# Asking for four experts' weights at other places of one DMA queue

## The chip, the cores and the metric

The kernel runs on one core of one Trainium2 chip. The metric is device time in microseconds (us) for one execution; lower is better. Engines are named as in the profile: PE (TensorE matmuls), PEld (TensorE weight loads), DVE (VectorE), ACT (ScalarE), POOL (GpSimd) and SP (SyncE, which here does little but ask for DMAs). SPq and POOLq are the DMA-asking parts of SP and POOL.

## The reference, cut to what matters

```python
# 1. global filter: x is (8, 2496, 256)
X = np.fft.rfft(x, axis=1)
y = np.fft.irfft(X * (filt_r + 1j * filt_i)[None], n=2496, axis=1)
# 2. mixture of experts over all 19968 rows of y; 8 experts, capacity 80
logits = y @ w_gate
expert_idx = np.argmax(logits, axis=1)
gate_w = softmax(logits)[arange(N), expert_idx]
for e in range(8):
    tok = rows with expert_idx == e, the 80 with the largest gate_w
    h = np.maximum(y[tok] @ w1[e], 0.0)            # w1[e]: 256 x 1024
    out[tok] = gate_w[tok, None] * (h @ w2[e])     # w2[e]: 1024 x 256
```

All other rows of the output are zero. One expert's two weight matrices are 2 x 1024 KB in float32.

## The kernel before, in words

The Fourier transform is done by matmuls in two stages. For each of the 8 batches b the filtered spectrum is written to DRAM (`yf[b]`) and the gate's logits are computed from it. Only some rows of the inverse transform are ever needed, at most 80 for each expert, so the kernel first finds the kept rows (on DVE) and then inverts just those.

That is done in seven **inverse rounds**, the list `ROUNDS`, 0 to 6. A round makes 128 rows of `y`. Its left operand is a tile `wt`: rows of a table of cosines, fetched from DRAM by four indirect DMAs on POOL's queue (`gather_rows`, tile `gt`, L852) and transposed on DVE (`turn_rows`, L863). Its right operand is a **page**, the spectrum of one batch, read back from `yf` by `load_page` (four DMAs, L837). Round r below 4 uses page r. Rounds 4 to 6 are cut into four groups of 32 rows: round 4 uses pages 4 and 5, round 5 pages 5 and 6, round 6 page 6 and the last batch's spectrum, which never left the core. `fill(n)` writes n of a round's 20 steps to PE (L875): one matmul of 128 columns a step in rounds 0 to 3, four of 32 columns from round 4 on. When a round's last step is done, `fill` copies the result on ACT to a tile `yr` (L881; round 5 goes to the tile `z`) and asks on SP's queue for its store to `y_sel` in DRAM (L882). `yr` has a single buffer, so the next round's copy waits for the store before it.

The eight experts come last. The rows of each are gathered from `y_sel` (L1155 for the first two, L1182 for the others, on POOL's queue), turned on PE, and run through `layer1` (L1215, `ph`) and `layer2` (L1235, `po`), then turned back (L1251), scaled by the gate on ACT (L1260) and scattered to the output (L1171).

`load_weights(e)` asks on SP's queue for expert e's weights with two DMAs, w1 (L1064) and w2 (L1066), below w0, w1, ... for expert 0, 1, ... as a whole. The five tiles that hold them are mostly the places of pages: w0 has a place of its own, w1 takes page 3's place, w2 page 4's, w3 page 5's, w4 page 6's; a request for one waits until the last round that reads the page is done. w5, w6 and w7 are asked for after layer 2 of experts 0, 1 and 2.

The order of the program text sets the order on every engine and queue (`tc.manual_schedule()`). SP takes its requests strictly one after the other: while one waits, all behind it wait.

## Time and profile before

| | us |
|---|---|
| median of 3 runs | 378.23 |
| lowest and highest run | 378.18, 383.19 |
| profiled execution, its own time | 379.92 |
| span of its trace | 378.1 |
| PE busy in the span | 351.0 (93%) |

The profiled execution took 1.69 us longer than the median, and 1.8 us of it lie outside the span. Times of day below ("at 288 us") count from the span's start. The inverse rounds fill some 235 to 318 us, the experts 318 to 370 us.

### The profile page before, as it was taken

Reading aid. Unit: us, or ns where it says so; the run is one execution under the profiler, and the core shown is the slowest. Engines: PE = TensorE matmul, PEld = TensorE weight load, DVE = VectorE, ACT = ScalarE, POOL = GpSimd, SP = SyncE. Lnnn points to the kernel's source line nnn. Section 1 sums busy time; section 2 is a strip of 40 time slices with the busy share of each in tenths; the row PEclk is TensorE's granted clock in tenths of the full one; section 3 lists DMA queues with packets and bytes.
Section 4 is the critical chain, followed back from the end, with each engine's and each line's share of the span. In section 5 each row is a group of like instructions: output and inputs, shape, how many; then the busy total and the mean of one; then the engine's idle time right before and its main releaser. Section 6 shows DMA issues by size and latency. Waiting matters only on the chain. (4 is left out here: it accounts for less than half of the span.)

```text
span 378.1 us, 9670 instructions
## 1 busy us (share of the span) xinstructions
PE 351.0 (93%) x3941; PEld 311.2 (82%) x3941; DVE 240.1 (63%) x494; ACT 132.8 (35%) x275; POOL 181.3 (48%) x250
## 2 busy tenths in 40 slices
PE   8888999999999999999999998998897989897990
PEld 4788989989989899899899897697784756786880
DVE  6049666757868858879989889769959540111110
ACT  1545545454545454454444465140100000010110
POOL 8337555544655536636457858850085102223120
PEclk9999999999999999999999999999999999999997
DMA  7998699979988999989989999799999773999310
GB/s 220 287 324 275 190 341 291 341 253 316 344 257 291 332 317 309 372 235 285 353 286 279 395 298 341 261 404 392 413 398 408 272 248 70 346 366 368 106 33 12
DMA packets 41099, 109.92 MB, mean 291 GB/s; under 512 B 4202, under 2 KB 14312, under 8 KB 39176
## 3 DMA queue, kind: packets, MB, share of 16 engines
q1 hardware_dynamic: 36534, 95.94, 74.7%
q0 software_dynamic: 4240, 13.15, 9.6%
q8 instruction: 33, 0.54, 0.6%
q10 hardware_dynamic: 274, 0.14, 0.2%
q14 instruction: 18, 0.15, 0.1%
HBM read 70.42 MB, written 40.37 MB: 293 GB/s over the span
## 5 line engine op out<-in xcount | busy, mean ns | idle before, releaser
L359 POOL TENSOR_TENSOR yt<-p 128x256 f32<-128x256 f32 x156 | 113.3, 748 | 89.7 <-DVE p L351 86.4
L351 DVE TENSOR_TENSOR p<-pb,ft 128x1024 f32<-128x1024 f32 x80 | 96.9, 1214 | 39.2 <-issue 17.9
L316 PE MATMUL pa<-wf_t,x 117*128 117x120 f32 x704 | 90.5, 275 | 2.5 <-DMA x<-in_x_dram 2.5
L316 PEld LDWEIGHTS pa<-wf_t,x 117*128 117x128 f32 x704 | 84.6, 192 | 3.7 <-issue 1.9
L341 PE MATMUL pb<-d_t,t 128*128 128x128 f32 x640 | 84.7, 275 | 1.7 <-ACT t L334 1.7
L341 PEld LDWEIGHTS pb<-d_t,t 128*128 128x128 f32 x640 | 77.7, 192 | 2.2 <-ACT t L334 2.2
L321 ACT COPY tt<-pa 128x480 f32<-128x480 f32 x96 | 47.8, 515 | 78.2 <-PE pa L316 76.0
L875 PE MATMUL pr<-page,wt 128*32 128x256 f32 (+1 forms) x520 | 63.9, 380 | 2.1 <-issue 2.1
L875 PEld LDWEIGHTS pr<-page,wt 128*32 128x32 f32 (+1 forms) x520 | 46.1, 134 | 15.7 <-issue 3.8
L334 ACT COPY t<-pt 128x512 f32<-128x512 f32 x80 | 47.2, 589 | 15.6 <-PE pt L330 13.8
L330 PE MATMUL pt<-ident,tt 128*128 128x128 f32 x320 | 48.6, 274 | 0.4 <-ACT tt L321 0.4
L372 DVE STREAM_TRANSPOSE u<-yt 128x512 f32<-128x512 f32 x70 | 48.9, 699 | 0.0
L852 POOL DMA_INDIRECT gt<-rows_tbl,idxr x28 | 29.4, 1052 | 33.7 <-DVE idxr L694 19.0
L330 PEld LDWEIGHTS pt<-ident,tt 128*128 128x128 f32 x320 | 37.2, 142 | 1.9 <-issue 1.2
L863 DVE STREAM_TRANSPOSE wt<-gt 128x640 f32<-128x640 f32 x28 | 22.4, 827 | 8.2 <-DMA gt<-rows_tbl,idxr 8.1
L1215 PE MATMUL ph_True<-xs_True,w 128*64 128x80 f32 x512 | 20.7, 234 | 1.5 <-issue 1.5
L395 PE MATMUL pz<-yt,wg 128*32 128x512 f32 (+1 forms) x256 | 21.7, 436 | 0.4 <-POOL yt L359 0.4
L1171 POOL DMA_INDIRECT out_dram<-ys_True,idxs x7 | 6.5, 933 | 31.7 <-ACT ys_True L1260 31.7
L1235 PE MATMUL po_True<-hT_True,w 128*64 128x80 f32 x448 | 18.3, 235 | 3.5 <-issue 3.5
L1215 PEld LDWEIGHTS ph_True<-xs_True,w 128*64 128x64 f32 x512 | 19.2, 137 | 2.4 <-issue 2.3
L881 ACT COPY yr<-pr 128x256 f32<-128x256 f32 x6 | 2.3, 379 | 53.6 <-DMA y_sel<-yr 38.4
L1235 PEld LDWEIGHTS po_True<-hT_True,w 128*64 128x64 f32 x448 | 16.6, 137 | 4.7 <-issue 4.2
(226 smaller groups left out, 287.6 us busy)
## 6 DMA issues: line engine op xcount, KB each, us to landing
out_dram<-zero_t SPq DMA_DIRECT2D x32, 624.0 KB
yf<-u SPq DMA_DIRECT2D x56, 320.0 KB
w<-in_moe_w_dram SPq DMA_DIRECT2D x16, 1024.0 KB
page<-yf SPq DMA_DIRECT2D x24, 640.0 KB
x<-in_x_dram SPq DMA_DIRECT2D x16, 936.0 KB
x<-in_x_dram SPq DMA_DIRECT2D x7, 702.0 KB
page<-yf POOLq DMA_DIRECT2D x4, 640.0 KB
fst<-in_filt_r_dram SPq DMA_DIRECT2D x10, 128.0 KB
```

Of the source, the lines that this page charges most:

```text
L316: nc.tensor.matmul(out=ps[:, j, :], rhs=wf_t, start=True, stop=True, lhsT=xt[3 * b + ch][:, j0 + j - JC * ch, 128 * cb:128 * cb + 128])
L321: nc.scalar.copy(out=tt[h][:, :, H3 * j0:H3 * j0 + hn * jn].rearrange("p s (j h) -> p s j h", h=hn), in_=v)
L330: nc.tensor.transpose(ps[:, i, :], tt[h][:, 2 * s:2 * s + 2, :].rearrange("p r n -> p (r n)"), ident[:])
L334: nc.scalar.copy(out=t2[k][:], in_=ps[:])
L341: nc.tensor.matmul(out=ps[:, :, i, :], lhsT=t[:, i, :], rhs=d_t[:, SG * g + i, :], start=True, stop=True)
L351: nc.vector.tensor_tensor(out=p[:], in1=f.unsqueeze(2).to_broadcast(shape), op=AL.mult, in0=ps[:].rearrange("p r s q -> p r (s q)").unsque ...
L359: eng.tensor_tensor(out=y[:, :, 2 * r:2 * r + 2, :], in0=a, in1=b, op=op)
L372: nc.vector.transpose(uu[h][:, :, SG * g:SG * g + SG, :].rearrange("p a s w -> p s a w"), spectrum(h)[:, SG * g:SG * g + SG])
L852: nc.gpsimd.indirect_dma_start(out=gts[b, g][:].rearrange("p s q -> p (s q)"), out_offset=None, in_=quarters, in_offset=bass.IndirectOffse ...
L875: nc.tensor.matmul(st["po"][c:c + w, :], lhsT=wts[r][:, s, c:c + w], rhs=yt_t[:, :, s] if b == B - 1 else columns(pages[b], s), start=(s = ...
L1215: nc.tensor.matmul(ph[c:c + 64, i, 0:cap], lhsT=w1[:, k, f:f + 64], rhs=xs[:, k, :], start=(k == 0), stop=(k == NDB - 1))
L1235: nc.tensor.matmul(po[c:c + 64, d, 0:cap], lhsT=w2[:, fc, 128 * d + c:128 * d + c + 64], rhs=hT[:, fc, :], start=(fc == 0), stop=(fc == NF ...
```

## The change

Three calls of `load_weights` move in the program text; nothing is added or taken away. The request for w0 moves from in front of round 0 to behind round 3, w1's from behind page 5 to behind round 4, and w3's from behind round 6 to behind the store of round 5. w2 and w4 keep their place.

```diff
         load_page(3, last)
-        load_weights(0)
         for g in range(3):
...
         fill(13)
         load_page(5, pg_p)
-        load_weights(1)
         turn_last(7)
...
         fill(20)
+        load_weights(0)
         turn_all(4)
...
         fill(20)
+        load_weights(1)
         load_weights(2)
...
         fill(10)
+        load_weights(3)
         turn_all(6)
...
         fill(20)
-        for e in (3, 4):
-            load_weights(e)
+        load_weights(4)
```

SP's queue, the only engine whose order changes, from the request for page 3 to the request for w2, before. The rows of L1064 and L1066 are w0, w1 and w2 in turn, those of L882 the stores of rounds 0 to 4, the two L837 rows after the first are pages 4 and 5:

```order
L837 DMA page_2954<-yf_148 128x1280 x4
L1064 DMA w_2959<-in_moe_w_dram 128x2x1024
L1066 DMA w_2959<-in_moe_w_dram 128x8x256
L882 DMA y_sel<-yr_3103 128x256
L837 DMA page_3106<-yf_149 128x1280 x4
L882 DMA y_sel<-yr_3228 128x256
L837 DMA page_3231<-yf_150 128x1280 x4
L1064 DMA w_3236<-in_moe_w_dram 128x2x1024
L1066 DMA w_3236<-in_moe_w_dram 128x8x256
L882 DMA y_sel<-yr_3404 128x256
L882 DMA y_sel<-yr_3458 128x256
L882 DMA y_sel<-yr_3588 128x256
```

The same stretch after:

```order
L837 DMA page_2954<-yf_148 128x1280 x4
L882 DMA y_sel<-yr_3100 128x256
L837 DMA page_3103<-yf_149 128x1280 x4
L882 DMA y_sel<-yr_3225 128x256
L837 DMA page_3228<-yf_150 128x1280 x4
L882 DMA y_sel<-yr_3398 128x256
L882 DMA y_sel<-yr_3452 128x256
L1064 DMA w_3455<-in_moe_w_dram 128x2x1024
L1066 DMA w_3455<-in_moe_w_dram 128x8x256
L882 DMA y_sel<-yr_3585 128x256
L1064 DMA w_3588<-in_moe_w_dram 128x2x1024
L1066 DMA w_3588<-in_moe_w_dram 128x8x256
```

Pages 4 and 5 and the stores of rounds 0 to 3 now stand ahead of all weights; w0 stands between the stores of rounds 3 and 4, w1 behind that of round 4, and w2 right behind w1.

The end of the same queue before, from w2 on; `z` is the store of round 5, the `yr` behind it that of round 6, and `bad` is a flag that every engine reads for the branch at the end:

```order
L1064 DMA w_3591<-in_moe_w_dram 128x2x1024
L1066 DMA w_3591<-in_moe_w_dram 128x8x256
L1377 TENSOR_LOAD bad
L1377 ISA x2
L882 DMA y_sel<-z 128x256
L882 DMA y_sel<-yr_3844 128x256
L1064 DMA w_3847<-in_moe_w_dram 128x2x1024
L1066 DMA w_3847<-in_moe_w_dram 128x8x256
L1064 DMA w_3850<-in_moe_w_dram 128x2x1024
L1066 DMA w_3850<-in_moe_w_dram 128x8x256
```

And after:

```order
L1064 DMA w_3591<-in_moe_w_dram 128x2x1024
L1066 DMA w_3591<-in_moe_w_dram 128x8x256
L882 DMA y_sel<-z 128x256
L1064 DMA w_3748<-in_moe_w_dram 128x2x1024
L1066 DMA w_3748<-in_moe_w_dram 128x8x256
L1377 TENSOR_LOAD bad
L1377 ISA x2
L882 DMA y_sel<-yr_3847 128x256
L1064 DMA w_3850<-in_moe_w_dram 128x2x1024
L1066 DMA w_3850<-in_moe_w_dram 128x8x256
```

w3 now stands between the stores of rounds 5 and 6, and the read of the flag comes behind it.

## Rows read from the trace of the kernel before

**Rows 1.** The page: busy time of PE and of its weight loads, share of the span and instructions; then tenths in 40 slices of 9.45 us (PEclk is the granted TensorE clock, DMA the share of the DMA engines); then the queue that brings instructions: packets, MB, share.

```profile
PE 351.0 (93%) x3941; PEld 311.2 (82%) x3941; DVE 240.1 (63%) x494; ACT 132.8 (35%) x275; POOL 181.3 (48%) x250
...
PEclk9999999999999999999999999999999999999997
DMA  7998699979988999989989999799999773999310
...
q8 instruction: 33, 0.54, 0.6%
```

**Rows 2.** Busy time by stretch, 239 to 370 us: stretch, its length, then busy us and instructions of PE, PEld, DVE, ACT and POOL, granted clock, DMA share, GB/s.

```profile
248.00:260.00 12.00, 10.74 (x66) 9.47 (x66) 9.75 (x28) 5.35 (x11) 3.50 (x4) 1.00 1.02 401
260.00:268.00 8.00, 7.98 (x47) 6.94 (x46) 7.23 (x38) 0.00 (x0) 0.00 (x0) 1.00 1.05 392
...
286.00:292.00 6.00, 3.87 (x62) 1.95 (x54) 5.36 (x17) 0.00 (x0) 3.63 (x4) 1.00 1.03 406
...
303.00:306.00 3.00, 1.94 (x25) 1.28 (x29) 1.73 (x6) 0.37 (x1) 0.00 (x0) 1.00 0.30 92
306.00:312.00 6.00, 6.00 (x119) 3.63 (x112) 2.83 (x6) 0.37 (x1) 0.00 (x0) 1.00 0.98 344
312.00:318.00 6.00, 6.00 (x116) 3.49 (x106) 0.00 (x0) 0.00 (x0) 1.91 (x2) 1.00 0.16 46
...
321.00:327.00 6.00, 4.68 (x114) 4.13 (x110) 0.49 (x1) 0.87 (x2) 2.83 (x3) 1.00 0.99 340
327.00:331.00 4.00, 4.00 (x111) 3.82 (x108) 1.14 (x3) 0.00 (x0) 0.00 (x0) 1.00 1.03 341
331.00:352.00 21.00, 17.93 (x437) 16.70 (x433) 3.55 (x10) 3.19 (x8) 5.75 (x6) 1.00 1.06 364
```

**Rows 3.** SP's queue in order of time: start, us (how long the request was held), what; the rows of L1064 and L1066 are w0, w1, w2, then w5.

```profile
244.13 0.40 SPq L1064 DMA_DIRECT2D w<-in_moe_w_dram  x1
...
254.40 7.04 SPq L882 DMA_DIRECT2D y_sel<-yr  x1
261.55 1.93 SPq L837 DMA_DIRECT2D page<-yf  x4
...
285.73 0.38 SPq L1064 DMA_DIRECT2D w<-in_moe_w_dram  x1
...
304.74 0.39 SPq L1064 DMA_DIRECT2D w<-in_moe_w_dram  x1
...
330.07 0.37 SPq L1064 DMA_DIRECT2D w<-in_moe_w_dram  x1
```

**Rows 4.** ACT's copies of rounds 1 and 3: start, us, what, and in brackets the idle time before it and what ended it.

```profile
268.36 0.37 ACT L881 COPY yr<-pr 128x256 f32<-128x256 f32 x1 [12.31 <-DMA y_sel<-yr]
...
301.68 0.37 ACT L881 COPY yr<-pr 128x256 f32<-128x256 f32 x1 [24.17 <-DMA y_sel<-yr]
```

**Rows 5.** PE in round 4, order of time, the last two of its three waits there: start, us, what, number of matmuls, and the idle time before with what ended it ("issue" where the profile shows nothing).

```profile
290.12 0.42 PE L875 MATMUL pr<-page,wt 128*32 128x256 f32 x2 [0.83 <-issue]
291.56 6.24 PE L875 MATMUL pr<-page,wt 128*32 128x256 f32 x107 [1.03 <-issue]
```

**Rows 6.** PE from the first turn of an expert's rows to layer 1 of experts 0 and 1, the same columns; the last and longest of the four waits there.

```profile
318.04 0.45 PE L1193 MATMUL px_True<-ident,xg_first 80*128 80x80 f32 x2
...
320.38 2.57 PE L1215 MATMUL ph_True<-xs_True,w 128*64 128x80 f32 x66
...
325.35 1.96 PE L1215 MATMUL ph_True<-xs_True,w 128*64 128x80 f32 x50 [0.43 <-issue]
```

**Rows 7.** PE in experts 1 to 4, the same columns: the five rows with a wait.

```profile
335.09 0.64 PE L1235 MATMUL po_True<-hT_True,w 128*64 128x80 f32 x13 [0.42 <-issue]
...
336.10 2.30 PE L1215 MATMUL ph_True<-xs_True,w 128*64 128x80 f32 x59 [0.17 <-issue]
...
341.70 0.78 PE L1235 MATMUL po_True<-hT_True,w 128*64 128x80 f32 x17 [1.02 <-issue]
...
348.32 0.98 PE L1235 MATMUL po_True<-hT_True,w 128*64 128x80 f32 x22 [1.47 <-issue]
...
354.06 1.19 PE L1235 MATMUL po_True<-hT_True,w 128*64 128x80 f32 x28 [0.59 <-issue]
```

**Rows 8.** Busy time by stretch, from the end of one wait of rows 7 to the end of the next; columns as in rows 2.

```profile
335.09:341.70 6.61, 5.43 (x127) 4.98 (x127) 1.08 (x3) 0.91 (x2) 2.13 (x3) 1.00 1.06 368
341.70:348.32 6.62, 5.15 (x127) 4.87 (x127) 1.08 (x3) 0.91 (x2) 2.07 (x3) 1.00 1.05 360
348.32:354.06 5.74, 5.14 (x127) 4.86 (x127) 1.08 (x3) 0.91 (x2) 1.08 (x2) 1.00 0.73 253
```

**Rows 9.** DMA queues in the stretches 339.0 to 339.5, 345.5 to 346.0 and 351.5 to 352.0, in this order: the row of the queue that brings instructions (packets, MB, share).

```profile
q8 instruction: 1, 0.02, 14.5%
...
q8 instruction: 1, 0.02, 15.5%
...
q8 instruction: 1, 0.02, 13.1%
```

**Rows 10.** POOL's queue, order of time: the first of three gathers for round 6 that follow each other during round 4, the gather for expert 0, and the first of three for experts 2 to 4.

```profile
286.95 1.00 POOL L852 DMA_INDIRECT gt<-rows_tbl,idxr  x1 [0.30 <-DVE hit L725]
...
314.92 0.96 POOL L1155 DMA_INDIRECT xg_first<-y_sel,idxg  x1 [17.46 <-DMA y_sel<-z]
...
321.15 0.94 POOL L1182 DMA_INDIRECT xg_True<-y_sel,idxg  x1 [4.01 <-PE px_True L1195]
```

## The prediction, made before the changed kernel was run

> **What bounds the kernel now.** I read the page first: PE is busy 93% of the span at a granted clock that is full almost everywhere [rows 1], and the DMA engines run at 0.7 to 0.9 or more in nearly every slice. So I looked for the places where PE, the busy engine, waits, and for what. The table by stretch [rows 2] is the second view. From 248 to 268 us the DMA engines are full (1.02 and 1.05) and PE still runs: 10.74 of 12.00 us, then 7.98 of 8.00. The stretches that stand out are 286 to 292 (PE 3.87 of 6.00), 321 to 327 (4.68 of 6.00) and 331 to 352 (17.93 of 21.00), with a full DMA in all three. In the order of time [rows 5, 6, 7] none of the waits there is for data: each reads "issue", nothing that the profile can name.
>
> The waits of 331 to 352 have a pattern. From the wait that ends at 335.09 to that at 341.70, from there to 348.32 and on to 354.06, PE runs 127 matmuls and as many weight loads each time [rows 7, 8]. One packet of the instruction queue lies in each of these stretches, two to three us before PE goes on [rows 9]. The page has 33 such packets with 0.54 MB, 16 KB each, for 3941 matmuls and as many weight loads [rows 1], 239 of these instructions to a packet, which agrees with 127 matmuls and their loads. I take it that PE stands still because its next block of instructions comes late when the weights fill the DMA engines. From 312 to 318, with the DMA at 0.16, PE does not wait; but from 306 to 312, in rounds 5 and 6 with the DMA at 0.98 from w2, it does not wait either (6.00 of 6.00) [rows 2]. The reason that I see is pace: there 119 matmuls take 6 us, one block lasts over 6 us; in the experts a block lasts some 5 us (5.15 busy of 6.62) [rows 8].
>
> The waits of rows 5 and 6 look different: a few matmuls, a pause, a few more. Both lie in a full DMA just after POOL has begun to ask for three gathers in a row (286.95 and 321.15) [rows 10]. I have no cause for them.
>
> **The change part by part.** All 2 x 1024 KB of each expert are still moved. At the 364 GB/s of 331 to 352 [rows 2] that is 5.8 us of full DMA for each.
>
> *w0 leaves the stretch before 268.* It is asked for at 244.13, and the store of round 0 behind it is held 7.04 us, so that page 4 is asked for at 261.55 only [rows 3]. Without it page 4 goes out up to 7 us sooner, page 5 some 3 us, since round 1's copy on ACT (268.36) had waited for that store [rows 4]. PE gets nothing: it hardly waited from 260 to 268 (7.98 of 8.00) [rows 2]. Term: 0. DVE waits less for gathers in rounds 4 and 5, which is worth nothing while PE is behind it.
>
> *w0 takes w1's place.* Round 3 ends at 285.7, when w1 was asked for [rows 3]; now w0 goes out there, about 1 us later, behind a store. The stream of pages and gathers in front of it is shorter by one expert's 5.8 us. The first use of w0 is at 320.38 [rows 6], over 30 us later. The pauses of round 4 cost 6.00 - 3.87 = 2.13 us of idle PE [rows 2, 5]; the same three gathers and again a new stream of weights meet there, so I leave them as they are: 0, with bounds of 2.13 gained and, from the other such place, 6.00 - 4.68 = 1.32 lost [rows 2, 6].
>
> The Trainium skill ("DMA: Bandwidth & Descriptors", Rules for kernel authors) speaks against this part: it says to ask for a DMA early, compute, and wait for it late. By that rule the later request costs whatever of the transfer is then seen; the trace leaves it over 30 us of cover, so the sum would be the same 0.
>
> *w1 joins w2 behind round 4.* Both go out at about 298.5 instead of 285.73 and 304.74 [rows 3]. They make 11.6 us of full DMA, to some 310, where the share was down to 0.30 from 303 to 306 [rows 2]. PE is in rounds 5 and 6 then. The nearest row is 306 to 312: same rounds, full DMA, no wait. Term: 0; bound above: three blocks of instructions pass from 299 to 320, each late by up to the 1.02 of rows 7, so 3.1 us lost.
>
> *w3 goes out behind round 5*, at about 310.5, into the stretch 312 to 318 whose share was 0.16. Behind it on SP wait the flag's read and round 6's store, which is ready only when the first turn has begun (318.04) [rows 6], after w3's 5.8 us. Round 5's store now queues behind w1 and w2 instead of w2; both orders are through by 310 to 312, so the first gather (314.92) [rows 10] is no later, and its rows are first used at 318.04 [rows 6]. Term: 0.
>
> *What is left for the experts.* In the kernel before, w3 and w4 start together at 319 to 321 and run without a break into w5, w6 and w7 until 352. Now w4 alone runs, 321 to 327. From 327 to w5's data, a little after its request at 330 [rows 3], the DMA rests, where the share was 1.03 [rows 2]. A block of instructions that PE asks for there comes in time: the waits that end at 335.09 and 336.10 go, 0.42 + 0.17 = 0.59 us. From then on w5, w6 and w7 follow each other as before, one each 6.6 us with 5.8 us of stream [rows 8]: the waits of 1.02 and 1.47 stay. The stream ends earlier, since w5 no longer queues behind w3 and w4, by two to three us; then the last wait, 0.59, goes too. The pauses of rows 6 fall in 321 to 325, when one weight stream and three gathers run in both orders: they stay, bound 1.32 gained.
>
> Sum: 0.59 + 0.59 = 1.2 us gained. Against the profiled execution's own 379.92 that gives 378.7; taken from the median, 378.23 - 1.2 = **377.0 us**.
>
> **The rivals.**
>
> *Nothing moves: 378.2 us.* The waits are not from the DMA's load, or they only change places. For it: PE never waits for a byte of weights or pages in these stretches, and the amount of DMA stays the same. Against it: the four waits of rows 7 sit in the full stretch, and none in 312 to 318. The Trainium skill ("Runtime: NRT & Kernel Launch", Instruction fetch mechanics) says that engines take their instructions in 16 KiB blocks, the next while one runs, and that crossing a block is mostly hidden. The block's size agrees with the page's 0.54 MB in 33 packets; that it is hidden does not agree with the 1.02 and 1.47 us of rows 7.
>
> *The pauses go too: 374.7 us.* If the pauses in round 4 and in layer 1 need a queue as deep as before (pages, w0's backlog and w1; w3 with w4 behind it), they shrink: up to 2.13 + 1.32 = 3.45 us more than my sum, 373.6 us at best; two thirds of it gives 374.7. For it: w0's 5.8 us are gone from the backlog at 288. Against it: the share of the DMA, not the depth, is what the rows show, and it stays full.
>
> *Slower: 380.7 us.* Rounds 5 and 6 lose what the experts lost. From 298 to 318 the DMA is now full for 17 of 20 us. The block of instructions must come within the 6 to 7 us in which PE uses one up; in the experts it took about 5 + 1.47 us at the worst [rows 7, 8]. If w1 and w2 together, asked for without a pause, make it 8 us, each of three blocks is late by 1 to 1.5 us: 3 to 4 us lost, less the 1.2 gained, 380.0 to 381.1. It decides at a delay of some 6.5 us, and the trace has that value on the edge. For it: that edge. Against it: the quiet of 306 to 312 with w2 alone.
>
> **How the numbers follow.** Forecast (375.5 to 378.0): 0.45. Nothing moves (378.0 to 378.6): 0.18. Pauses go (372.5 to 375.5): 0.17. Slower (378.6 to 382): 0.20. The range leaves out the lower third of the third case and a little under half of the last, with some allowance for several effects at once: 373.4 to 380.6. A change of 2% is 7.6 us, and about what a measurement here tells from no change. All the idle PE of rows 5 to 7 together is 2.13 + 1.32 + 3.67 = 7.1 us, less than that, so faster by over 2% needs more than everything: 0.03. Slower by over 2% needs a stage to wait for its weights, which have tens of us of cover: 0.03. Within 2%: 0.94.
>
> **What would show it.** In the changed profile: page 4 asked for at about 255 and round 3's copy at about 286 instead of 301.68; DMA share near 1 from 298 to 310, high from 312 to 318, and low from 327 to 331; in PE's order of time no "issue" wait near 335 and a smaller one near 354, still two of 1 us or more between; pauses in round 4 and in layer 1 as before. I am wrong if PE shows "issue" waits between 299 and 318 (the slower rival), if the pauses of round 4 vanish (the faster one), or if layer 1 of an expert waits for its weights, which no part of the sum has.

## The result, and the profile after

The changed kernel is **slower: 1.0063 times the time before, interval 1.0042 to 1.0084**; medians 382.19 us and 379.55 us, 20 runs each. The kernel before took 379.55 in these runs and not the 378.23 from which the prediction started; on that base the ratio gives 380.6 us. The forecast was 377.0, a gain of 1.2 us, so the sign is wrong. The change moves three requests, w0, w1 and w3, not the four of the title. Runs over 1.5% longer than the fastest of the same kernel are left out of the ratios. The profiled execution took 382.2 us, its span is 380.4.

The two traces of the prediction's places, and one more execution of each kernel (its times in the last column), cut at the starts of matmuls:

| stretch | before | after | difference | second pair |
|---|---|---|---|---|
| start of the span to round 0 | 235.56 | 234.82 | -0.74 | +0.93 |
| round 0 to the last matmul of round 6 | 82.17 | 80.56 | -1.61 | -0.87 |
| from there to the first turn of an expert's rows | 0.31 | 4.63 | **+4.32** | **+4.17** |
| first turn to layer 2 of expert 0 | 9.09 | 9.62 | +0.53 | +0.57 |
| layer 2 of expert 0 to the last matmul group | 38.54 | 36.66 | -1.88 | -1.42 |
| last matmul group to the end | 12.46 | 14.12 | **+1.66** | **+1.32** |
| span | 378.1 | 380.4 | +2.3 | +4.7 |

The first row is the same work in both kernels and shows how much two executions differ. Of the two gains, that of the experts was foreseen and that of the rounds put at 0; the two losses are where nothing was looked for.

Of the page, the rows of [rows 1]: PE is as busy as before, and the granted clock has a dip in the two slices of 314 to 333 us.

```profile
PE 352.1 (93%) x3941; PEld 311.6 (82%) x3941; DVE 241.6 (64%) x494; ACT 133.1 (35%) x275; POOL 180.5 (47%) x250
...
PEclk9999999999999999999999999999999998799997
```

Busy time by stretch after, columns as in [rows 2]:

```profile
286.00:292.00 6.00, 6.00 (x116) 3.61 (x112) 4.28 (x14) 0.00 (x0) 2.53 (x3) 1.00 1.02 403
292.00:298.00 6.00, 4.62 (x74) 2.41 (x70) 4.15 (x16) 0.37 (x1) 0.99 (x1) 1.00 1.04 380
...
306.00:312.00 6.00, 6.00 (x120) 3.60 (x112) 0.49 (x2) 0.37 (x1) 0.00 (x0) 1.00 1.02 363
312.00:316.00 4.00, 3.76 (x72) 1.99 (x64) 0.00 (x0) 0.10 (x1) 0.97 (x1) 1.00 0.99 353
316.00:320.00 4.00, 0.00 (x0) 0.02 (x1) 0.00 (x0) 0.27 (x1) 0.95 (x1) 1.00 0.78 216
320.00:323.00 3.00, 2.99 (x16) 3.00 (x16) 0.33 (x1) 0.00 (x0) 1.69 (x2) 0.57 1.03 390
323.00:327.00 4.00, 4.00 (x58) 3.85 (x59) 0.33 (x1) 0.44 (x1) 1.15 (x2) 0.50 0.70 213
327.00:331.00 4.00, 4.00 (x110) 3.91 (x107) 0.98 (x2) 0.44 (x1) 0.00 (x0) 0.97 0.00 0
```

The quiet stretch of the kernel before, 312 to 318 at a share of 0.16 [rows 2], is gone: 0.99. Then PE does nothing for four microseconds, and the seven after them run at a granted clock of 0.57 and 0.50, the lower of its two levels (1.2 GHz). The rest comes at 327 to 331 instead, where the share is 0.00.

What PE waits for there, in its order of time (columns as in [rows 5]); the first row is round 4, the next two round 5, the fourth the first turn, the last two experts 2 and 3:

```profile
285.76 7.09 PE L875 MATMUL pr<-page,wt 128*32 128x256 f32 x128
...
294.49 0.62 PE L875 MATMUL pr<-page,wt 128*32 128x256 f32 x2 [0.37 <-DVE wt L863]
296.13 4.50 PE L875 MATMUL pr<-page,wt 128*32 128x256 f32 x74 [1.02 <-DVE wt L863]
...
320.01 0.42 PE L1193 MATMUL px_True<-ident,xg_first 80*128 80x80 f32 x2 [4.25 <-DMA xg_first<-y_sel,idxg]
...
323.24 6.56 PE L1215 MATMUL ph_True<-xs_True,w 128*64 128x80 f32 x128
...
342.60 0.78 PE L1235 MATMUL po_True<-hT_True,w 128*64 128x80 f32 x17 [0.58 <-issue]
...
349.49 0.98 PE L1235 MATMUL po_True<-hT_True,w 128*64 128x80 f32 x22 [1.74 <-issue]
```

4.25 us before the first turn, for the gather of the first experts' rows. How the gather came late is in two queues. SP's queue after (as [rows 3]; page 4, w0, then the store of round 5 and the first half of w3 behind it):

```profile
253.12 1.80 SPq L837 DMA_DIRECT2D page<-yf  x4
...
285.05 0.40 SPq L1064 DMA_DIRECT2D w<-in_moe_w_dram  x1
...
307.62 0.34 SPq L882 DMA_DIRECT2D y_sel<-z  x1
308.05 0.39 SPq L1064 DMA_DIRECT2D w<-in_moe_w_dram  x1
```

and POOL's two gathers for experts 0 and 1 after (as [rows 10]):

```profile
314.96 0.97 POOL L1156 DMA_INDIRECT xg_first<-y_sel,idxg  x1 [17.62 <-DMA y_sel<-z]
316.23 0.95 POOL L1156 DMA_INDIRECT xg_first<-y_sel,idxg  x1 [0.30 <-issue]
```

The same three requests before, from SP's and from POOL's queue:

```profile
309.96 0.34 SPq L882 DMA_DIRECT2D y_sel<-z  x1
```

```profile
316.19 0.95 POOL L1155 DMA_INDIRECT xg_first<-y_sel,idxg  x1 [0.30 <-issue]
```

Round 5's result is stored 2.34 us earlier than before (307.62 for 309.96), yet the first gather, which waits for the store, goes out at 314.96 as it did at 314.92: the store takes 7.34 us to the gather instead of 4.96. The landings in the trace say why these two times agree: in both kernels the store stands behind w2 and lands 0.34 to 0.36 us after w2's second half (before 313.70 and 314.06, after 313.76 and 314.10). w1, in front of w2, had landed at 307.63.

From the second gather's request to the first turn it is 3.78 us instead of 1.85, and PE, 2.35 us ahead by then, has run out of work. The 1.85 is only a bound, since PE was busy until then. The packets of POOL's queue show the gathers themselves, 48 packets for each, from the first one's request to 317.30, before and then after:

```profile
q0 software_dynamic: 48, 0.07, 11.5%
```

```profile
q0 software_dynamic: 32, 0.05, 7.8%
```

Before, the first gather is complete by 317.27, 2.35 us after its request and some 0.8 us before PE needs it; after, its last part lands at 319.88, 4.92 us after its request, beside w3.

The second loss is in the last scatters, each of which waits for the one before it to land. After, POOL's last three scatters, and ACT's results for the last two of them:

```profile
363.22 0.91 POOL L1171 DMA_INDIRECT out_dram<-ys_True,idxs  x1 [3.01 <-ACT ys_True L1260]
367.27 0.91 POOL L1171 DMA_INDIRECT out_dram<-ys_True,idxs  x1 [3.14 <-DVE hT_True L1221]
372.26 0.91 POOL L1171 DMA_INDIRECT out_dram<-z,idxs  x1 [4.08 <-POOLq L1383]
```

```profile
365.19 0.47 ACT L1260 ACTIVATE ys_True<-pb_True,gate 80x256 f32<-80x256 f32 x1
370.01 0.47 ACT L1260 ACTIVATE z<-po_True,gate 80x256 f32<-80x256 f32 x1 [4.35 <-PE po_True L1244]
```

and POOL's three before:

```profile
362.60 0.91 POOL L1171 DMA_INDIRECT out_dram<-ys_True,idxs  x1 [3.08 <-ACT ys_True L1260]
365.68 0.91 POOL L1171 DMA_INDIRECT out_dram<-ys_True,idxs  x1 [2.17 <-ACT ys_True L1260]
370.13 0.91 POOL L1171 DMA_INDIRECT out_dram<-z,idxs  x1 [3.54 <-ACTq L1383]
```

The requests stand 4.05 and 4.99 us apart instead of 3.08 and 4.45, and the last one goes out 1.78 us after its rows are ready (370.48). No weights move in that stretch.

### The profile page after: what moved, and what is told of

Its sections match the earlier page's. It is cut to its first block, busy times and chain, and to the rows that moved or that the text cites. A ratio compares the mean times of both kernels' runs of the same rounds, so it can differ in the third digit from the quotient of the medians.

```text
span 380.4 us, 9670 instructions
## 1 busy us (share of the span) xinstructions
PE 352.1 (93%) x3941; PEld 311.6 (82%) x3941; DVE 241.6 (64%) x494; ACT 133.1 (35%) x275; POOL 180.5 (47%) x250
## 5 line engine op out<-in xcount | busy, mean ns | idle before, releaser
L875 PEld LDWEIGHTS pr<-page,wt 128*32 128x32 f32 (+1 forms) x520 | 44.5, 134 | 16.5 <-DVE wt L863 2.3
L395 PE MATMUL pz<-yt,wg 128*32 128x128 f32 (+1 forms) x256 | 21.6, 436 | 0.4 <-POOL yt L359 0.4
L1215 PEld LDWEIGHTS ph_True<-xs_True,w 128*64 128x64 f32 x512 | 20.4, 148 | 0.3 <-issue 0.2
L395 PEld LDWEIGHTS pz<-yt,wg 128*32 128x32 f32 x256 | 8.7, 109 | 12.3 <-issue 7.0
```

The lines of the kernel that those rows point to most:

```text
L395: nc.tensor.matmul(out=ps[32 * j:32 * j + 32].rearrange("p (s w) -> p s w", s=pn), lhsT=wg[:, cb, :], rhs=yt_t[:, (2 * b + cb) % 2, 5 * j ...
L875: nc.tensor.matmul(st["po"][c:c + w, :], lhsT=wts[r][:, s, c:c + w], rhs=yt_t[:, :, s] if b == B - 1 else columns(pages[b], s), start=(s = ...
L1215: nc.tensor.matmul(ph[c:c + 64, i, 0:cap], lhsT=w1[:, k, f:f + 64], rhs=xs[:, k, :], start=(k == 0), stop=(k == NDB - 1))
```

## The experiments

**The theory** after the result: w3 took the quiet of 312 to 318 from the chain store of round 5, gather, first turn. **Rivals:** the store queues behind the weights on SP and would be quick on another queue; w2, not w3, is what delays it; w0 or w1 at their new places cost the time; the drop of the clock, not the wait, is the price. All times of the table are from the profiled execution, the ratios from the runs (of e13 and e14 there is one each). "Store" is from the request of round 5's store to the first gather, "gather" from the second gather's request to the first turn (where "turn" is 0.31 or 0.35, PE was busy until then, and the gather may have landed earlier), "turn" from the last matmul of round 6 to the first turn, "end" from the last matmul group to the end of the span.

| kernel | ratio to before | store | gather | turn | end |
|---|---|---|---|---|---|
| before | 1 | 4.96 | 1.85 | 0.31 | 12.46 |
| after | 1.0063 [1.0042, 1.0084] | 7.34 | 3.78 | 4.63 | 14.12 |
| e1_z_act | 1.0069 [1.0036, 1.0102] | 6.87 | 4.85 | 5.23 | 14.13 |
| e2_w2_late | 1.0091 [1.0060, 1.0122] | 2.64 | 5.91 | 2.06 | 13.41 |
| e3_busy | 1.0033 [1.0003, 1.0063] | 8.49 | 4.14 | 6.14 | 13.73 |
| e4_w3_back | 1.0039 [1.0011, 1.0067] | 6.66 | 1.36 | 1.53 | 13.77 |
| e5_only_w0 | 1.0215 [1.0181, 1.0249] | 6.75 | 1.35 | 1.60 | 13.89 |
| e6_only_w1 | 1.0016 [0.9987, 1.0046] | 5.31 | 1.49 | 0.31 | 12.58 |
| e7_only_w3 | 1.0060 [1.0028, 1.0093] | 4.99 | 4.93 | 3.12 | 12.58 |
| e8_quiet | 1.0038 [1.0008, 1.0068] | 2.60 | 4.31 | 0.31 | 14.06 |
| e9_pool6 | 1.0081 [1.0050, 1.0111] | 7.22 | 3.80 | 4.53 | 12.46 |
| e10_act6 | 1.0037 [1.0003, 1.0071] | 7.78 | 3.80 | 5.10 | 12.59 |
| e11_dve6 | 1.0033 [1.0001, 1.0065] | 6.90 | 3.83 | 4.24 | 12.60 |
| e12_pe20 | 1.0120 [1.0074, 1.0166] | 6.23 | 5.06 | 4.80 | 12.60 |
| e13_after | (383.97 us) | 6.42 | 4.56 | 4.48 | 13.78 |
| e14_before | (379.26 us) | 4.87 | 2.08 | 0.31 | 12.46 |
| e15_w3_back_dve6 | 1.0021 [1.0001, 1.0042] | 5.46 | 1.38 | 0.35 | 12.46 |

### Which part of the change it is

**w3 alone** (the kernel before, with w3 behind round 5):

```diff
+        load_weights(3)
         turn_all(6)
...
-        for e in (3, 4):
-            load_weights(e)
+        load_weights(4)
```

> The kernel before with w3's request alone moved, to behind the store of round 5. Rounds 3 and 4 are untouched, so round 6 ends near 318 as before. Theory C: w3 now runs from about 311 to 318 beside the gather of the first experts, whose rows come 2 to 3 us later than in the kernel before; PE waits 2 to 4 us before the first turn and may fall to the lower clock: 1 to 4 us more than the kernel before. If only the depth of the queue in front of round 5's store counts (w1 and w2), nothing is lost here, and the wait near 335 goes: 0.5 to 1.5 us less than the kernel before.

Measured 1.0060. POOL's second gather and PE's first turn of this kernel, and its busy time by stretch:

```profile
315.54 0.96 POOL L1156 DMA_INDIRECT xg_first<-y_sel,idxg  x1 [0.30 <-issue]
```

```profile
320.47 0.42 PE L1193 MATMUL px_True<-ident,xg_first 80*128 80x80 f32 x2 [2.75 <-DMA xg_first<-y_sel,idxg]
```

```profile
312.00:316.00 4.00, 4.00 (x84) 2.40 (x76) 0.00 (x0) 0.00 (x0) 1.43 (x2) 1.00 0.90 328
...
322.00:325.00 3.00, 3.00 (x39) 2.85 (x39) 0.33 (x1) 0.00 (x0) 2.39 (x3) 0.50 1.03 380
```

The store takes as long as before (4.99): it lands 0.40 us behind w2, which was asked for at 304 as before. The gather meets w3's stream (share 0.90) and takes 4.93 us instead of at most 1.85. PE waits 2.75 us, and its clock falls behind the wait. By its ratio, one moved line costs as much as all three.

**w3 back, w0 and w1 moved** (the changed kernel without its w3 line):

```diff
         fill(10)
-        load_weights(3)
         turn_all(6)
...
-        load_weights(4)
+        for e in (3, 4):
+            load_weights(e)
```

> The changed kernel with w3's request back behind round 6: w0 and w1 alone are moved against the kernel before. Theory A: the store of round 5 still stands behind w1 and w2 and lands near 313 to 315, so the wait before the first turn stays for the most part (2.5 to 4 us; the gather itself lands 1 to 2 us sooner, because w3 does not run beside it), with the lower clock after it: within 1.5 us of the changed kernel. If w3 beside the gather is what makes it late, the wait goes and the time falls by 3 us or more.

Measured 1.0039. The gather is quick again (1.36), so the share of w3 in its delay is confirmed from the other side; the time fell by less than the 3 us expected for this. The store is still slow (6.66) and again lands 0.36 us behind w2 (313.76 and 314.12). PE's first turn:

```profile
317.61 0.42 PE L1193 MATMUL px_True<-ident,xg_first 80*128 80x80 f32 x2 [1.15 <-DMA xg_first<-y_sel,idxg]
```

The gain in the experts is gone as well: waits of 0.72, 0.33, 0.91, 1.19 and 0.59 us, and 38.48 us from layer 2 of expert 0 to the last group. w3 alone doesn't bring it either (38.23); it takes the moves together. What remains of the loss must have another place; the end (13.77) is one.

**w1 alone** (the kernel before, with w1 behind round 4):

```diff
-        load_weights(1)
         turn_last(7)
...
         fill(20)
+        load_weights(1)
         load_weights(2)
```

> The kernel before with w1's request alone moved, to behind round 4 in front of w2. Theory C: w1 and w2 are through by about 305 to 307, the chain from the store of round 5 to the first turn stays quick (store 2.5 to 4 us, PE's wait under 1 us, no lower clock); with round 4's pauses gone too, 1 to 3 us less than the kernel before. If the pauses of round 4 need w0's early place to go: no change within 1 us.

Measured 1.0016, its interval spans 1: no loss that can be told from no change, and not the 1 to 3 us less that were expected; the pauses of round 4 stay. Rounds 5 and 6 run beside w1 and w2 without an "issue" wait.

**w0 alone** (the kernel before, with w0 behind round 3, hence behind w1 on SP's queue):

```diff
-        load_weights(0)
         for g in range(3):
...
         fill(20)
+        load_weights(0)
         turn_all(4)
```

> The kernel before with w0's request alone moved, to behind round 3 (there it stands behind w1 and the stores of rounds 2 and 3); w3 stays behind round 6. Theory C (what is lost is the quiet of the DMA engines from 307 to 318: the store of round 5, the gather of the first two experts behind it and PE's first turn are one chain, and each link is late beside weights): weights are through by about 306 here, so the store lands in 2.5 to 3.5 us, the gather in about 2, PE waits under 1 us before the first turn at full clock, and what round 4 gained (some 2 us) is kept: 1 to 2.5 us less than the kernel before. Rival D (the gain of round 4 comes from w1 leaving the place beside rounds 4's gathers, not from w0): round 4's pauses stay and the time is that of the kernel before within 1 us.

Measured 1.0215, far more than w0 costs in the changed kernel: here w1, still behind page 5, goes out first, the stores of rounds 2 and 3 behind it go out at 286.01 and 300.65, and w0 leaves SP only at 301.16. So this run doesn't measure w0's part of the change. Its profiled execution (383.34 us) was some 4 us quicker than the other runs, and what the others lost more isn't in its trace.

### What the delay is

**The store on another queue** (the changed kernel):

```diff
-                    nc.sync.dma_start(
+                    (nc.scalar if r == NR - 2 else nc.sync).dma_start(
```

> The changed kernel, with the store of round 5 alone asked for on ACT's queue instead of SP's, so that it no longer stands behind w1 and w2. Theory A (PE stands 4.25 us before the first turn because that store lands late behind w1 and w2, and then runs some 6.8 us at the lower clock): the gather for expert 0 goes out near 311 instead of 314.96, PE's wait before the first turn falls under 1 us, the granted clock stays at 1.00 from 320 to 327, and the time falls by 4 to 6 us against the changed kernel, below the kernel before by 2 to 4 us. Theory B (the loss is in the experts' own waits for instructions and in the tail): PE's wait before the first turn may go, but the time stays within 1.5 us of the changed kernel's, since the pauses in layer 1 come back at full clock.

Measured 1.0069, as after. ACT's queue and POOL's first gather:

```profile
307.48 0.36 ACTq L882 DMA_DIRECT2D y_sel<-z  x1
```

```profile
314.35 0.96 POOL L1156 DMA_INDIRECT xg_first<-y_sel,idxg  x1 [17.15 <-DMA w<-in_moe_w_dram]
```

The store leaves at once on a queue of its own and still takes 6.87 us. The row names w2, which landed last before the gather (313.68); what POOL's wait ended with is the store's own landing at 313.49. So its place behind w2 in SP's queue isn't what holds it: on either queue it is late while w2 is being moved.

**w2 behind round 5's store, with w3** (the changed kernel):

```diff
         load_weights(1)
-        load_weights(2)
...
         fill(10)
+        load_weights(2)
         load_weights(3)
```

> The changed kernel, with w2's request moved from behind w1 to behind the store of round 5 and in front of w3, everything on SP's queue. Theory A: the store of round 5 lands some 2.5 us after its request, as round 6's does, PE does not wait before the first turn or well under 2 us (the gather runs beside w2 and w3), no stretch at the lower clock, 3 to 6 us less than the changed kernel. Theory B: no change of more than 1.5 us against the changed kernel; with w2, w3 and w4 together behind round 5 the experts' waits for instructions grow instead.

The store is now quick, 2.64 us, so w2 was what held it. But the 2 x 5.8 us of weights behind it now meet the gathers: asked for at 309.10 and 310.37, they are there 5.91 us after the second request, and the one for expert 2 is late as well:

```profile
316.28 0.42 PE L1193 MATMUL px_True<-ident,xg_first 80*128 80x80 f32 x2 [1.68 <-DMA xg_first<-y_sel,idxg]
...
329.02 0.53 PE L1198 MATMUL px_True<-ident,xg_True 80*128 80x80 f32 x2 [2.68 <-DMA xg_True<-y_sel,idxg]
```

PE's clock is low behind both waits (0.57 in 318 to 322, 0.58 in 328 to 332). 1.0091 instead of the 3 to 6 us less that were expected: the wait has only moved on along the chain.

**Both behind round 6** (the changed kernel with w2 and w3 after the gathers):

```diff
         load_weights(1)
-        load_weights(2)
...
-        load_weights(3)
         turn_all(6)
...
-        load_weights(4)
+        for e in (2, 3, 4):
+            load_weights(e)
```

> The changed kernel with w2 and w3 both moved to behind the store of round 6, in front of w4: w0 behind round 3, w1 behind round 4, and no weights from about 302 to 318. Theory C: the store of round 5 lands in 2.5 to 3 us, the gather is out by 312 and in by 315, PE does not wait before the first turn and keeps the full clock; some 2 us gained there against the kernel before. Behind it w2, w3 and w4 run together from 318 to 336, so the pauses and waits of the experts stay or grow by up to 2 us: 2 us less to 1 us more than the kernel before, 3 us or more below the changed kernel. If the wait before the first turn stays although nothing runs beside the chain, theory C falls.

With no weights beside it the chain is quick: the store takes 2.60 us, the gathers are there before PE has done round 6, and PE doesn't wait:

```profile
313.37 0.97 POOL L1154 DMA_INDIRECT xg_first<-y_sel,idxg  x1 [14.13 <-DMA y_sel<-z]
```

```profile
318.95 0.45 PE L1192 MATMUL px_True<-ident,xg_first 80*128 80x80 f32 x2
```

The ratio is 1.0038 all the same, not the 3 us or more below the changed kernel that were expected. The trace (384.56 us, above the median of 381.74) shows pauses in round 4 and in layer 1 like those of [rows 5, 6], and the long end (14.06). Behind the pauses of layer 1, none over 0.47 us in its rows, with PE busy for 2.73 of the 4.00 us from 322 on, the granted clock falls too:

```profile
326.00:330.00 4.00, 3.68 (x60) 3.69 (x62) 0.49 (x1) 0.44 (x1) 0.00 (x0) 0.58 1.09 342
```

So freeing the chain mends the chain, not the kernel.

**PE kept at work** (the changed kernel with four matmuls of 512 columns behind round 6, which compute nothing that is used):

```diff
+        warm2 = mps.tile([128, 4, 128], F32, name="warm2", tag="m")
+        for _ in range(4):
+            nc.tensor.matmul(warm2[:], lhsT=ident[:], start=True, stop=True,
+                             rhs=ident[:].unsqueeze(1).to_broadcast([128, 4, 128]))
```

> The changed kernel with four matmuls of 512 columns on constants added on PE right behind round 6, where it waits for the gather; they write a tile that nobody reads. They take about 3.4 us of the 4.25. Theory A with its second half: the gather comes no earlier, but the granted clock stays at 1.00 behind it, so 2 to 3 us less than the changed kernel (layer 1 of experts 0 and 1 in about 5 us instead of 6.56). If the clock has no part: no change, or up to 0.5 us more.

The gather comes as late as after. Busy time by stretch (from an execution of 383.39 us, the median is 380.70):

```profile
316.00:319.00 3.00, 3.00 (x8) 1.04 (x6) 0.00 (x0) 0.00 (x0) 1.72 (x2) 1.00 0.89 253
...
324.00:327.00 3.00, 3.00 (x28) 2.85 (x30) 0.32 (x1) 0.00 (x0) 0.95 (x1) 0.52 0.60 181
327.00:328.00 1.00, 1.00 (x28) 1.00 (x26) 0.00 (x0) 0.02 (x1) 0.00 (x0) 0.75 0.02 6
```

The low clock lasts about half as long. 1.0033 against 1.0063 would put about half of the loss on the clock, but the intervals overlap, and e10 below comes to 1.0037 with a low clock from 320 to 331. What the clock costs in the whole time isn't shown.

### The long end

In the first ten kernels of the table (before to e8) the end is short in those that ask for w0 in front of round 0 and long in all others, though no weights move in it. In the changed kernel a packet of the instruction queue lies at 364.5 us, between the request of the scatter of 363.22 and its data; before, it lies behind the data. The theory was that this packet belongs to one engine whose blocks of instructions fall otherwise after the change. Four kernels shift the instructions of one engine each: the changed kernel with six writes of one element on POOL, six copies on ACT, six writes on DVE, or twenty matmuls of 32 columns on PE, all behind round 6 and used by nothing.

```diff
         fill(20)
+        spare = near_p.tile([1, 8], F32, name="spare")
+        for i in range(6):
+            nc.gpsimd.memset(spare[:, i:i + 1], 0.0)
         load_weights(4)
```

> The changed kernel with six one-element writes added to POOL's order behind the gathers for experts 0 and 1, where POOL waits anyway. They move POOL's later instructions by six against the 16 KB blocks in which instructions are fetched, and nothing else. In the changed kernel the end, from the last matmul group's start (366.29) to the end of the span (380.4), takes 14.1 us, before it took 12.5, and a packet of the instruction queue falls 5.1 us ahead of the last matmul's start, between the request of the last-but-two scatter (6.37 ahead) and its data; before, it fell 4.4 us ahead, behind that data. Theory 'the packet holds the scatter up, and it is POOL's': the packet moves by more than 0.3 us or leaves, the end shrinks to 12.4 to 12.8, the time by 1 to 1.6 us to 380.6 to 381.2. Theory 'another engine's packet': packet at 5.1 ahead, end 13.7 to 14.1, time 381.7 to 382.7.

On ACT the loop writes a copy instead:

```diff
+            nc.scalar.activation(out=spare[:, i:i + 1], in_=ident[0:1, i:i + 1],
+                                 func=AF.Copy)
```

> The changed kernel with six one-element copies added to ACT's order behind round 6, so that ACT's later instructions stand six further in their blocks. Theory 'the packet is ACT's': the packet 5.1 us ahead of the last matmul's start moves by more than 0.3 us, the end shrinks from 14.1 to 12.4 to 12.8 us, the time to 380.6 to 381.2. Theory 'another engine's packet': end 13.7 to 14.1, time 381.7 to 382.7.

On DVE:

```diff
+            nc.vector.memset(spare[:, i:i + 1], 0.0)
```

> The changed kernel with six one-element writes added to DVE's order behind round 6. Theory 'the packet is DVE's': the packet 5.1 us ahead of the last matmul's start moves by more than 0.3 us, the end shrinks from 14.1 to 12.4 to 12.8 us, the time to 380.6 to 381.2. Theory 'another engine's packet': end 13.7 to 14.1, time 381.7 to 382.7.

And on PE, in place of the writes:

```diff
+        warm2 = mps.tile([128, 4, 128], F32, name="warm2", tag="m")
+        for _ in range(20):
+            nc.tensor.matmul(warm2[:, 0, 0:32], lhsT=ident[:], rhs=ident[:, 0:32],
+                             start=True, stop=True)
```

> The changed kernel with twenty matmuls of 32 columns (forty instructions with their weight loads) added to PE's order behind round 6, where PE waits 4.25 us for the gather. PE's later blocks then begin twenty matmuls earlier in the work. Theory 'the packet is PE's': the packet 5.1 us ahead of the last matmul's start moves to about 5.9 (twenty matmuls of some 40 ns, 5.15 us for 127 of them), ahead of or at the start of the scatter's data at 4.9 to 4.8; the end changes by over 0.5 us. Theory 'another engine's packet': the packet stays at 5.1 and the end at 13.7 to 14.1; the time is that of the changed kernel, 381.7 to 382.7, or up to 1.1 less if the matmuls keep the clock up, as the four larger ones did.

**All four** have the short end, 12.46 to 12.60 us. (Each added matmul stands twice in the trace, so e12 adds forty to PE, not twenty.) POOL's last three scatters with the writes on DVE:

```profile
364.75 0.92 POOL L1174 DMA_INDIRECT out_dram<-ys_True,idxs  x1 [3.08 <-ACT ys_True L1263]
367.86 0.92 POOL L1174 DMA_INDIRECT out_dram<-ys_True,idxs  x1 [2.19 <-ACT ys_True L1263]
372.28 0.92 POOL L1174 DMA_INDIRECT out_dram<-z,idxs  x1 [3.50 <-ACTq L1386]
```

3.11 and 4.42 us apart, as before. Each of the four theories expected that of one kernel only, so the theory that one engine's blocks alone decide it falls. Nor do more instructions always do it: e3, with four larger matmuls on PE, keeps the long end (13.73).

What the theory said of the packet itself holds in all seventeen traces. DMA queues after, in 364.40 to 364.60 (the instruction packet) and in 365.25 to 366.00 (the last three of the 48 packets of the scatter asked for at 363.22); then before, in 364.00 to 364.55 (all 48 of the scatter of 362.60) and in 364.55 to 364.75 (the instruction packet):

```profile
q8 instruction: 1, 0.02, 29.0%
...
q0 software_dynamic: 3, 0.01, 4.9%
```

```profile
q0 software_dynamic: 48, 0.08, 51.3%
...
q8 instruction: 1, 0.02, 31.5%
```

After, the instruction packet starts 0.22 us ahead of the scatter's data; fifteen of the scatter's sixteen parts land by 365.53, the last one at 366.50. Before, it starts 0.52 us behind the start of the data, and all parts land by 364.90. In the eight traces with a long end the packet starts between 0.30 us ahead of that scatter's data and 0.05 us behind its start, and the last part lands 0.90 to 1.60 us behind the fifteenth; in the nine with a short end it starts 0.49 us or more behind, or (e12) 1.7 us ahead, and the last part lands within 0.13 us. In all seventeen the next scatter goes out 0.77 us after the last part. So the end goes with the packet's place in every trace; that the packet is what holds the late part up is read from these times, not tested apart. In e12, the only one that adds to PE's order, it moves by 1.46 us, about forty matmuls of 40 ns, which leans to a block of PE's. Why six instructions on POOL, ACT or DVE move it by 0.7 to 0.8 us isn't shown.

The times don't follow the end: e10 and e11 lie about 1 us under the changed kernel (ten runs each), e9 and e12 above it (four runs each). These four differ from the changed kernel only by idle work, and lie from 1.0033 to 1.0120. So a difference of some 0.4% between two rows of the table doesn't show by itself what a moved request costs; the waits in the traces do.

Does the end belong to the program or to the execution? Both kernels once more, as they are:

> The changed kernel itself, once more. Adding a few instructions to POOL, ACT, DVE or PE shortened the end (last matmul group to end of span) from 14.1 to 12.5 or 12.6 us in all four, so no single engine's packet explains it. Theory 'the end belongs to the program, by how its blocks of instructions fall': 13.4 to 14.2 us again here. Theory 'the end varies between executions or chips': 12.4 to 12.7 here is possible, and as likely as not. The wait for the gather, 3.5 to 4.5 us before the first turn, is there under both.

> The kernel before itself, once more. Theory 'the end belongs to the program': 12.4 to 12.7 us. Theory 'it varies between executions or chips': 13.4 to 14.2 is possible. No wait for the first gather under both; the pauses of round 4 may be there or not.

13.78 and 12.46: to the program, as far as two executions of each tell. The wait for the gather is there again too (4.11 us), and the second pair's column in the first table is from these two. But **the pauses of round 4 differ between executions of one kernel**. Busy time in 286 to 292 of the changed kernel's second execution, where the first had 6.00, and of the kernel before, which had 3.87:

```profile
286.00:292.00 6.00, 5.59 (x69) 2.35 (x65) 4.63 (x15) 0.31 (x1) 4.05 (x4) 1.00 1.01 392
```

```profile
286.00:292.00 6.00, 4.42 (x60) 2.05 (x56) 5.44 (x16) 0.00 (x0) 2.99 (x3) 1.00 1.03 403
```

In the second execution of the changed kernel PE has 69 matmuls there, hardly more than the 62 of the kernel before, and not 116: the row takes most of its pauses for busy time. From round 0 to the end of round 4 it took 61.40 us, before 62.17, the first execution 57.96. Over all traces, round 4 (from its first matmul to the first of L747) took 8.77 us in five (after, e1 to e4) and 11.4 us or more in all others. All five have w0 and w1 moved, as have seven of the others: the pauses went only where both were moved, and not always there. What decides it isn't shown.

Last, both losses taken away: the changed kernel with w3 back behind round 6 and the six writes on DVE.

```diff
         fill(10)
-        load_weights(3)
         turn_all(6)
...
-        load_weights(4)
+        spare = near_p.tile([1, 8], F32, name="spare")
+        for i in range(6):
+            nc.vector.memset(spare[:, i:i + 1], 0.0)
+        for e in (3, 4):
+            load_weights(e)
```

> The changed kernel with w3 put back behind round 6, and the six one-element writes on DVE that went with a short end. If the loss of the change has two parts, the gather that comes late beside w3 and the long end, both are taken away here: PE waits under 1.5 us for the first gather, the end is 12.4 to 12.7 us, and the time is that of the kernel before, ratio 0.996 to 1.001 (w3 back alone, with the long end, gave 1.0039). If w0 and w1 behind rounds 3 and 4 cost something of their own elsewhere, ratio 1.002 to 1.006 with the short end too.

1.0021 [1.0001, 1.0042]: turn 0.35, end 12.46, granted clock full. The middle lies just above the 0.996 to 1.001 of two losses taken away, the interval reaches into it. Of the 0.63% some two thirds are gone by these numbers. What is left has no place of its own that I could name; the experts' waits are back (0.44, 0.74, 1.04 and 0.87 us), as in the kernel before.

## Why the prediction was wrong, step by step

**The step that failed: "*w3 goes out behind round 5* ... the first gather (314.92) [rows 10] is no later, and its rows are first used at 318.04 [rows 6]. Term: 0."** The first gather was no later, but it had to be earlier, since PE was; and the step took the request for the landing. It costed w3 by its own first use and the store of round 6 behind it, and named the quiet stretch of 312 to 318 only as room for w3. That room was in use: in the quiet the gathers took at most 1.85 us from the second request to the turn, beside w3 they take 3.78 to 5.06 (nine traces, after and e7 among them), and with w3 back 1.36 (e4). PE waits 4.25 us for them, where the term was 0. No part of the sum, nor a rival, had this wait; the rows for it (the store at 309.96, the gather at 316.19, the turn at 318.04) were in the trace of before, with 0.31 us between round 6 and the turn and some 0.8 us between the gather's landing (317.27) and the turn: next to no slack.

**"... both orders are through by 310 to 312, so the first gather (314.92) [rows 10] is no later"** held to the letter, 314.96, and hid the rest of the loss: round 5 was done and its store asked for 2.34 us sooner, and it spent them behind w2 in the DMA engines, whose second half landed at 313.76, before at 313.70. With w2 out of its way the store takes 2.64 us (e2), with all weights out of its way 2.60 (e8).

**w0 in front of round 0.** As foreseen: page 4 went out at 253.12 (foreseen 255) instead of 261.55, round 3's copy at 284.16 (286) instead of 301.68, and up to round 4 PE got little for it (round 0 to the start of round 4: 49.19 and 50.03 us after, 50.06 and 50.02 before).

**w0 in w1's place, the pauses.** The term was 0; rounds 0 to 6 as a whole gained 1.61 us in the first pair of executions and 0.87 in the second, within its bound of 2.13. In the first execution the pauses of round 4 were gone, and part of the gain came back as waits for DVE's transposes (0.37 and 1.02); in the second most of them were there. That they would stay is what was predicted, and no run shows a reason for it, so where it held it was luck.

**w1 with w2 behind round 4.** Term 0 held: no "issue" wait between 299 and 318, in the changed kernel or with w1 alone (1.0016). The slower rival, at 380.7, is near the measured time for a reason that didn't occur. (Its own sum was off too: three blocks at 1 to 1.5 us are 3 to 4.5 us, so up to 381.5.) A time that agrees is no support for a mechanism.

**The experts.** The rest came where it was foreseen, at 327 to 331 with a share of 0.00; the waits of 335.09, 336.10 and 354.06 went, two stayed (0.58 and 1.74 for 1.02 and 1.47). Foreseen were 1.2 us, measured 1.88 and 1.42. In the second execution (e13) these two waits are not there either; six of 0.23 to 0.36 us stand in their place, in pairs with five or six matmuls between. The rule of the Trainium skill that I had set against the trace ("Runtime: NRT & Kernel Launch", Instruction fetch mechanics: the crossing of a block is mostly hidden) again doesn't agree with a wait of 1.74 us. But no wait follows the packet of 332.06, which came while the DMA rested (w5 was asked for at 332.49).

**The pauses of layer 1** weren't there in the changed kernel, whose layer 1 ran on the low clock: 128 matmuls in 6.56 us, where before the two of [rows 6] and the pauses between lasted from 320.38 to 327.31. So layer 1 took no longer than before: what the low clock cost it is no more than what the pauses had cost. The 0.53 us of the table are the turns, 0.89 us longer on the low clock, less 0.36 from layer 1 to layer 2.

**The end.** 1.66 us, foreseen nowhere. It goes with the program, in two executions of each kernel, and with the place of one instruction packet before the last scatters; what moves that packet is open.

The Trainium skill ("DMA: Bandwidth & Descriptors", Rules for kernel authors) says to issue a DMA early and wait for it late. For w3 this was done, and in this case's runs it cost 0.6% (e7). The measurement doesn't speak against the rule for the transfer itself; it says who else has to be asked.

## What to carry to other kernels

A stretch in which the DMA engines rest is free only if nothing short and waited for runs in it: before you fill it, list the small transfers there, the time from each one's request to its first use, and the slack of the engine that uses it. A price of zero for a moved bulk transfer needs this list for every chain that it passes, not only for the mover's own first use. And a wait of a microsecond that sits in one trace may belong to the execution; a second trace of the same kernel tells that before a term rests on it.

## What the runs showed of the hardware

- A small DMA on a queue of its own was no quicker beside full DMA engines: 6.87 us from store to gather on ACT's queue (e1), 7.34 and 6.42 on SP's (after, e13), 2.60 with no weights about (e8).
- After PE had stood still for 4.25 us the granted clock was 0.50 to 0.57 for the seven microseconds of work that followed; after 2.75 us (e7) it was 0.50 in 322 to 325. It fell without a long stand as well: 0.58 in 326 to 330 of e8, behind pauses of at most 0.47 us.
- Where an instruction packet (16 KB) started 0.22 us ahead of a small scatter's data, one of the scatter's sixteen parts landed 0.97 us behind the other fifteen (after); where it started behind the data, all landed together (before). The other fifteen traces agree.
